# A list scheduler places single instructions of the attention units and weight sums between the feed-forward steps of a fused HGRN2 and bilinear FFN kernel

## The chip, the cores and the metric

The kernel runs on one core of one Trainium2 chip. The metric is the device time of one execution, in microseconds (us). The profile is of one execution on the same kind of core. TensorE is called PE, VectorE DVE, ScalarE ACT, GpSimd POOL and SyncE SP, as the profile does.

## The reference

A gated linear recurrence runs over 4 batches x 8 heads, 768 tokens of 48 channels; its output, 3072 tokens of 384 channels, goes through a bilinear feed-forward block of 1536 inner channels.

```python
f = 1.0 / (1.0 + np.exp(-f_logit))
for t in range(S):
    state = f[:, :, t, :, None] * state + np.einsum('bhd,bhe->bhde', k[:, :, t], v[:, :, t])
    y[:, :, t] = np.einsum('bhd,bhde->bhe', q[:, :, t], state)
x = y.transpose(0, 2, 1, 3).reshape(B * S, H * D)
out = ((x @ w_a) * (x @ w_b)) @ w_out
```

The device computes in float32. The weights arrive as 64-bit numbers and are narrowed on the device.

## The kernel before

**Units.** The recurrence is cut into 16 units: a batch, a half of the tokens (384) and a group of four heads. Two units make a block of 384 tokens x 384 channels, `xT[blk]`, of which there are eight. For a unit, `front` makes the two sigmoids on ACT, an affine step on POOL (line 289), the scans of products of f and of its inverse on DVE (lines 294 and 304), and multiplies q and k by them (306, 307). Then PE and the other engines do `scores` (with a mask on DVE, 357), `turn` (transposes of k, copied out by ACT, 373), `gains` (sums into states by DVE, 405), `within` and `across` (copied out by ACT, 457), and SP's DMAs carry the result into `xT`.

**Feed-forward.** For the first two blocks, `up` makes 12 steps each of 6 matmuls for one 128-wide slice of both inner products, and `product` multiplies the halves. While these run, the 20 pieces of the weights are narrowed (`from_double`). For the other six blocks `up_triples` computes the same by a scheme with 15 products in place of 18 over sums of weights (`combine_w_ba`) and of inputs (`combine_x`): four passes j of 15 products, two matmuls each, into four PSUM banks `ps_f`; ACT copies a bank out (616, 597), or DVE adds it to an earlier copy (619). A bank is used several times in a pass, and its next product waits until the copy or the addition has read it. `down` multiplies two groups of 128 tokens by `w_out` with 7 sub-products in place of 8, over sums of weights (`combine_w_out`: t1 to t4) and of inputs (s1 to s4, by DVE); each sub-product is 6 matmuls, into halves x0, x1, m0, m1 of two banks. There are 12 such calls.

**The order.** All instructions are emitted in one program order by the source, and each engine runs its own in that order; semaphores hold an instruction until what it depends on has finished. The order is written out by hand. `rest` is a list of feed-forward steps; a counter `step` goes up by 1 for an `up` step or a third of a triple pass, and by 0.5 for a sub-product of `down`. A queue of pairs (due step, generator) holds the six parts of each unit's `slot` and the 22 parts of the weight sums; after each step, `beside()` emits the parts that are due, each as a whole. `combine_x` is emitted as a whole in the last `down` ahead of its triples, and `combine_w_out` after the last narrowing.

**The sums of weights.** `combine_w_out` is four DVE additions (674 to 677) into `spare`, where the narrowing kept its bits, and into `w_out`. `combine_w_ba` is six ACT copies (533), eleven DMAs that add on the way (539), issued by POOL, and four DVE additions (547).

Of the kernel before, what the change touches and what calls it, by code (L numbers as in the profile page):

```python
# [19 lines left out]
C = 128  # L20
# [14 lines left out]
def weight_pieces(w_ba, w_out, moe_w_a, moe_w_b, moe_w_out):  # L35

    w_b, w_a = (w_ba[:, i] for i in range(2))
    NKT, NFT, DM = w_ba.shape[2], w_out.shape[1], w_out.shape[2]
    for ft, n in [(0, 1)] + [(ft, 2) for ft in range(1, NFT - 1, 2)] + [(NFT - 1, 1)]:
        for dst, src in ((w_b, moe_w_b), (w_a, moe_w_a)):  # L40
            cols = slice(ft * 128, (ft + n) * 128)
            yield dst[:, :, cols], src.rearrange("(kt p) c -> p kt c", p=128)[:, :, cols], (NKT, n * 128)
    for ft in range(0, NFT, 2):
        rows = moe_w_out[ft * 128:(ft + 2) * 128]
        yield w_out[:, ft:ft + 2], rows.rearrange("(k p) c -> p k c", p=128), (2, DM)
# [84 lines left out]
def by_quotients(ctx, tc, q, k, f_logit, v, moe_w_a, moe_w_b, moe_w_out, out, ident, weights, bad):  # L130
# [89 lines left out]
    todo, raws, going = list(weight_pieces(w_ba, w_out, moe_w_a, moe_w_b, moe_w_out)), [], []  # L220
# [47 lines left out]

    live = {}
# [7 lines left out]
    def front(u):  # L277
# [5 lines left out]
        if u in FIRST:  # L283
            nc.scalar.activation(F, x, AF.Sigmoid)
        nc.scalar.activation(inv, x, AF.Sigmoid, bias=less, scale=-1.0, accum_out=tails[:, u:u + 1])  # L285
        if u not in FIRST:
            nc.scalar.activation(x, x, AF.Sigmoid)

        nc.gpsimd.tensor_scalar(inv, inv, EXP_K, 1.0, ALU.mult, ALU.add)  # L289
        yield  # L290
        none = zero.broadcast_to((128, BLK))
        for n in range(2):
            c = slice(n * BLK, n * BLK + BLK)
            nc.vector.tensor_tensor_scan(F[:, c], F[:, c], none, math.exp(MIDDLE), ALU.mult, ALU.add)
        nc.vector.tensor_tensor(held[:, u], products_of_f[u][:, :, BLK - 1], least, ALU.is_ge)
        yield

        start = sb2.tile([128, 2, NC - 1], FP32, tag="start", name="start")
        nc.vector.reciprocal(start, products_of_f[u].rearrange("p n (c m) -> p n c m", m=C)[:, :, 0:NC - 1, C - 1])
        for n in range(2):  # L300
            for c in range(NC):
                w = slice(n * BLK + c * C, n * BLK + c * C + C)
                first = start[:, n, c - 1:c] if c else math.exp(-MIDDLE)
                nc.vector.tensor_tensor_scan(inv[:, w], inv[:, w], none[:, 0:C], first, ALU.mult, ALU.add)  # L304
        yield
        nc.vector.tensor_tensor(halves(t["q"]), halves(t["q"]), F, ALU.mult)
        nc.vector.tensor_tensor(halves(t["k"]), halves(t["k"]), inv, ALU.mult)
        live[u] = {}
        yield


# [21 lines left out]
    def scores(u, spare=False):  # L333
# [3 lines left out]
        for n, c, o in each():  # L337
            for h in range(2):
                for p in range(2):
# [7 lines left out]
                    )  # L347
        at = sb1.tile([128, 2, BLK], FP32, tag="at", name="at")
# [12 lines left out]
    def turn(u, spare=False):  # L361
# [10 lines left out]
        if not spare:  # L372
            nc.scalar.copy(kT.rearrange("s n c x -> s n (c x)"), ps_x[:, :, 0:BLK])
        live[u]["kT"] = kT
        give_back(ps)

    def gains(u):
# [21 lines left out]
        for j in range(NJ - 1 if last else NJ):  # L399
            c, p = divmod(j, 2)  # L400
            new = ps_x[:, p, 0:2 * NC * D].rearrange("r (n c d) -> r n c d", n=2, c=NC)[:, :, c]
            if before is None:
                nc.vector.tensor_copy(st[:, j], new)
            else:
                nc.vector.tensor_tensor(st[:, j], before, new, ALU.add)
            before = st[:, j]
        before = live[u]["st"][-1]
        if not last:

            for n in range(2):  # L410
                end = products_of_f[u][:, n, BLK - 1:BLK]
                nc.vector.tensor_scalar(before[:, n], before[:, n], end, math.exp(-MIDDLE), ALU.mult, ALU.mult)
# [19 lines left out]
    def across(u):  # L432
# [19 lines left out]
        y = sb1.tile([128, 2 * NC, 2, SUB], FP32, tag="y", name="y")  # L452

        whole = [(0, 0, 0, 128)] if ps[0] is y_banks[0] else [(0, 0, 0, D), (0, R, R, D)]
        for p, e, r, rows in (*whole, (1, R, 0, D), (1, 0, R, D)):
            copy = nc.vector.tensor_copy if u in FIRST and p else nc.scalar.copy
            copy(y[r:r + rows, :, p], ps[p][e:e + rows, 0:BLK].rearrange("r (o m) -> r o m", m=SUB))
        give_back(ps)
        y = y.rearrange("r (n c) p m -> r n (c p m)", n=2)
# [22 lines left out]

    factors = []

    def up(blk, ft):

        x, ps = xT[blk], {}
        for nm, w in (("b", w_b), ("a", w_a)):
            ps[nm] = ps_f[idle.pop(0)]
            for kt in range(NKT):  # L490
                nc.tensor.matmul(  # L491
                    ps[nm][:, 0:BLK],
                    lhsT=w[:, kt, ft * 128:ft * 128 + 128],
                    rhs=x[:, kt],
                    start=kt == 0,
                    stop=kt == NKT - 1,
                )
        factors.append((blk, ft, ps))
# [16 lines left out]
    free = []  # L515

    def combine_w_ba():

# [11 lines left out]
        for to, sign, x in (  # L530
            (s[1], 1, a12), (s[0], 1, a21), (s[3], 1, a22), (s[4], -1, a33), (s[5], -1, a11), (s[2], 1, a12)
        ):
            nc.scalar.activation(to, x, AF.Copy, scale=float(sign))
            yield
        for to, x in (
            (s[1], a22), (s[0], a32), (s[3], a23), (s[4], a31), (s[5], a31), (s[2], a22),
            (s[1], a23), (s[3], a32), (s[4], a21), (s[5], a32), (s[2], a21),
        ):
            nc.gpsimd.dma_start(out=to, in_=x, accum_op=ALU.add)
            yield  # L540
        for to, x, y, op in (
            (a31, a11, a31, ALU.subtract),
            (a31, a31, a33, ALU.add),
            (a22, s[1], a31, ALU.subtract),
            (a22, a22, a13, ALU.add),
        ):
            nc.vector.tensor_tensor(to, x, y, op)
            yield

    def combine_x(blk):  # L550
# [7 lines left out]

        def op(to, x, y, op):
            nc.vector.tensor_tensor(to, x, y, op)  # L560

        op(s[:, 0:2], x[:, 0], b31.unsqueeze(1).broadcast_to((128, 2, HT)), ALU.add)
        op(v1, b21, u5, ALU.subtract)
        op(v6, b31, b21, ALU.subtract)
        op(b11, b11, b12, ALU.subtract)
        op(u1, b11, v6, ALU.add)
        op(r2, b22, b32, ALU.subtract)
        op(v2, b22, v1, ALU.subtract)
        op(v4, b22, b31, ALU.subtract)
        op(t2, b32, b31, ALU.subtract)  # L570
        op(b32, b12, b32, ALU.add)
        op(b21, b21, b22, ALU.subtract)
        nc.scalar.activation(b22, b22, AF.Copy, scale=-1.0)
# [4 lines left out]
        )  # L578

    def up_triples(blk):  # L580
# [3 lines left out]
        def times(ps, name, j, start=False):  # L584
# [9 lines left out]

        def finish(j, c, out, v):
            times(v, "v6", j)
            nc.scalar.copy(out[1, 0], v)
# [3 lines left out]
            nc.vector.tensor_tensor(to.rearrange("p g (k j) t -> p j g k t", k=NI)[:, j], a, b, ALU.mult)  # L601

        for j in range(NJ3):
# [11 lines left out]
            def copy(to, ps):  # L615
                nc.scalar.copy(to, ps)  # L616

            def add(k, i, ps):
                nc.vector.tensor_tensor(out[k, i], ps, out[k, i], ALU.add)  # L619

            times(v, "v1", j, True)
            copy(out[2, 0], v)
            if tail:
                finish(*tail)
            times(u, "u1", j, True)
            copy(out[1, 1], u)
            times(r, "r2", j, True)
            add(1, 1, r)
            times(v, "v2", j)
            copy(out[2, 1], v)  # L630
            times(u, "u2", j)
            copy(first[:, :, 1], u)
            yield
            times(t, "t1", j, True)
            times(v, "v3", j)
            copy(first[:, :, 0], v)
            nc.vector.tensor_tensor(c[:, :, 1:3, 1], c[:, :, 1:3, 1], first, ALU.add)  # L637
            times(u, "u3", j)
            copy(out[0, 1], u)
            times(r, "r3", j, True)  # L640
            add(2, 1, r)
            times(v, "v4", j)
            copy(second[:, :, 1], v)
            yield
            times(u, "u4", j)
            copy(out[0, 0], u)
            add(0, 0, t)
            times(v, "v5", j)
            copy(second[:, :, 0], v)
            nc.vector.tensor_tensor(c[:, :, 0], c[:, :, 0], second, ALU.add)  # L650
            times(u, "u5", j)
            add(2, 0, u)
            times(t, "t2", j)
            add(0, 1, t)
            tail = j, c, out, v
            if j == NJ3 - 1:
                finish(*tail)
            yield

# [672 lines left out]
```

## Time and profile before

| | |
|---|---|
| time, median of three runs | 636.44 us (634.92 to 636.75) |
| the profiled execution: its time, its span | 636.59 us, 634.9 us |
| PE busy in 0 to 80 us | 51.8 us |
| DVE additions 674 to 677 | 1.35, 1.36, 1.36, 1.98 us |
| DVE additions 547 | 4, of 1.22 us |
| DMA additions 539 | 11, 512 KB each, median 10.1 us from issue to landing |
| start of the first `down` sub-product, and of the triples | 147.9 us, 210.8 us |
| last matmul starts, last store is issued | 625.38 us for the last group, 627.97 us |

Span means first to last instruction; some 1.7 us of the execution's time lie outside it. A float32 matmul is recorded as two instructions, so a sub-product of six appears as x12. The rows of a stage table give for each stretch the busy time of each engine; where PE's falls short of the stretch's length, PE was idle. A wait is put down to the instruction that released the one waiting.

### The profile page before, as it was taken

To read this page: it belongs to the slowest core of one execution; us is meant where nothing else is said; L and a number is where in the kernel's file an instruction comes from. 1 tells how busy PE (TensorE), PEld (TensorE's weight loads), DVE (VectorE), ACT (ScalarE), POOL (GpSimd) and SP (SyncE) were. 2 spreads that over 40 slices of the span, in tenths; PEclk is the share of its full clock that TensorE was granted. 3 is DMA by queue.
4 is the path that set the end of the run, shared out by engine and by line. 5 is a ranking of instruction groups with operands and counts; after the bars stand their busy time and mean duration, and the time that the engine had idled before them with its cause. 6 is when DMAs were issued, how large, how long until landed. Compare 5 with 4: busy or idle time off the path is not lost.

```text
span 634.9 us, 13922 instructions
## 1 busy us (share of the span) xinstructions
PE 579.7 (91%) x5778; PEld 512.9 (81%) x5778; DVE 413.6 (65%) x762; ACT 273.6 (43%) x508; POOL 77.0 (12%) x69
## 2 busy tenths in 40 slices
PE   0759899999997999998999999998999999999995
PEld 0626555558997888897999999898999999999995
DVE  6768445487987578757695677847794455745741
ACT  5577499932321445334532255335431245134400
POOL 6244154552000000000000000000000000000000
PEclk9959999999998999999999999999999999999998
DMA  9886775089244403040131404031000100000000
GB/s 215 247 251 174 173 262 185 15 143 189 57 115 90 119 1 95 2 102 18 32 64 40 105 3 94 3 73 46 17 6 33 38 1 20 2 27 1 1 26 30
DMA packets 33337, 49.43 MB, mean 78 GB/s; under 512 B 3952, under 2 KB 25072, under 8 KB 33264
## 3 DMA queue, kind: packets, MB, share of 16 engines
q1 hardware_dynamic: 29984, 42.38, 24.7%
q0 software_dynamic: 2992, 5.77, 5.4%
q8 instruction: 47, 0.77, 0.5%
q10 hardware_dynamic: 288, 0.30, 0.2%
q14 instruction: 26, 0.21, 0.1%
HBM read 33.23 MB, written 4.72 MB: 60 GB/s over the span
## 4 chain that ended last, share of the span: by engine, by line
PE 52%; DVE 11%; ACT 4%; issue 2%; DVEq 0%; ACTq 0%
PE ps_f L586 32%; PE ps_f L697 15%; DVE inv L304 2%; DVE x_sums L560 1%; DVE sums L692 1%; PE ps_x L341 1%; PE ps_y L423 1%; DVE groups L560 1%; PE ps_x L369 1%; DVE sums L637 1%; DVE sums L619 1%; DVE groups L601 1%; ACT inv L285 1%; DVE xT L560 1%; PE ps_y L444 1%
## 5 line engine op out<-in xcount | busy, mean ns | idle before, releaser
L491 PE MATMUL ps_f<-xT,w_ba 128*128 128x384 f32 x288 | 98.4, 502 | 7.8 <-DVE w_ba L66 6.2
L491 PEld LDWEIGHTS ps_f<-xT,w_ba 128*128 128x128 f32 x288 | 55.3, 195 | 47.7 <-DVE w_ba L66 7.3
L616 ACT COPY sums<-ps_f 128x384 f32<-128x384 f32 x108 | 51.8, 480 | 72.0 <-PE ps_f L586 69.0
L616 ACT COPY groups<-ps_f 128x384 f32<-128x384 f32 x108 | 51.7, 479 | 62.8 <-PE ps_f L586 55.1
L586 PE MATMUL ps_f<-xT,w_ba 128*128 128x192 f32 x384 | 78.6, 333 | 0.0
L586 PEld LDWEIGHTS ps_f<-xT,w_ba 128*128 128x128 f32 x384 | 63.4, 190 | 4.8 <-ACT sums L616 2.4
L586 PE MATMUL ps_f<-x_sums,raw 128*128 128x192 f32 x288 | 57.1, 331 | 6.3 <-ACT groups L616 6.2
L586 PE MATMUL ps_f<-groups,w_ba 128*128 128x192 f32 x288 | 55.3, 328 | 4.6 <-DVE sums L619 4.6
L586 PEld LDWEIGHTS ps_f<-x_sums,raw 128*128 128x128 f32 x288 | 46.6, 190 | 9.5 <-ACT groups L616 8.0
L697 PE MATMUL ps_f<-w_out,sums 128*128 128x192 f32 x288 | 53.8, 338 | 0.0
L586 PEld LDWEIGHTS ps_f<-groups,w_ba 128*128 128x128 f32 x288 | 47.8, 190 | 6.4 <-DVE sums L619 6.4
L697 PE MATMUL ps_f<-w_out,groups 128*128 128x192 f32 x288 | 51.1, 327 | 0.6 <-DVE u L692 0.6
L697 PE MATMUL ps_f<-spare,sums 128*128 128x192 f32 x288 | 49.6, 328 | 1.3 <-DVE sums L692 1.2
L289 POOL TENSOR_SCALAR inv<-inv 128x768 f32<-128x768 f32 x14 | 13.7, 975 | 298.3 <-ACT inv L285 298.3
L697 PEld LDWEIGHTS ps_f<-w_out,sums 128*128 128x128 f32 x288 | 48.6, 196 | 0.7
L697 PEld LDWEIGHTS ps_f<-spare,sums 128*128 128x128 f32 x288 | 46.8, 190 | 2.5 <-issue 1.3
L697 PEld LDWEIGHTS ps_f<-w_out,groups 128*128 128x128 f32 x288 | 47.2, 190 | 1.3 <-DVE u L692 1.2
L56 POOL TENSOR_SCALAR sums<-sums 128x768 f32<-128x768 f32 (+1 forms) x20 | 40.9, 2045 | 51.2 <-ACT sums L54 49.4
L619 DVE TENSOR_TENSOR groups<-ps_f,groups 128x384 f32<-128x384 f32 x60 | 32.2, 552 | 17.6 <-ACT groups L616 16.2
L619 DVE TENSOR_TENSOR sums<-ps_f,sums 128x384 f32<-128x384 f32 x60 | 32.1, 551 | 15.1 <-PE ps_f L586 9.9
L586 PE MATMUL ps_f<-x_sums,w_ba 128*128 128x192 f32 x192 | 39.0, 326 | 0.0
L586 PE MATMUL ps_f<-xT,raw 128*128 128x192 f32 x192 | 39.0, 326 | 0.0
(129 smaller groups left out, 869.6 us busy)
## 6 DMA issues: line engine op xcount, KB each, us to landing
raw<-w_ba POOLq DMA_DIRECT2D x11, 512.0 KB, 10.1
q_in<-in_q_dram SPq DMA_DIRECT2D x32, 144.0 KB, 4.2
k_in<-in_k_dram SPq DMA_DIRECT2D x32, 144.0 KB, 3.4
v_in<-in_v_dram SPq DMA_DIRECT2D x16, 288.0 KB, 5.0
raw<-in_moe_w_out_dram SPq DMA_DIRECT2D x6, 768.0 KB, 4.2
out_dram<-o SPq DMA_DIRECT2D x24, 192.0 KB, 1.9
f_in<-in_f_logit_dram SPq DMA_DIRECT2D x28, 144.0 KB, 3.0
xT<-y SPq DMA_DIRECT2D x46, 72.0 KB, 2.2
```

The lines of the kernel that those rows point to most:

```text
L56: nc.gpsimd.tensor_scalar(h, h, HI_MAX, None, ALU.min)
L285: nc.scalar.activation(inv, x, AF.Sigmoid, bias=less, scale=-1.0, accum_out=tails[:, u:u + 1])
L289: nc.gpsimd.tensor_scalar(inv, inv, EXP_K, 1.0, ALU.mult, ALU.add)
L304: nc.vector.tensor_tensor_scan(inv[:, w], inv[:, w], none[:, 0:C], first, ALU.mult, ALU.add)
L341: nc.tensor.matmul(ps[h][SUB * p:SUB * p + SUB, o:o + SUB], lhsT=kf[r, tokens(n, c, p)], rhs=qf[r, tokens(n, c, p)], start=True, stop=True,)
L369: nc.tensor.transpose(ps[n][:, c * C:c * C + C], kf[:, o:o + C], ident)
L491: nc.tensor.matmul(ps[nm][:, 0:BLK], lhsT=w[:, kt, ft * 128:ft * 128 + 128], rhs=x[:, kt], start=kt == 0, stop=kt == NKT - 1,)
L560: nc.vector.tensor_tensor(to, x, y, op)
L586: nc.tensor.matmul(ps[:, g], lhsT=sums_of_w[name][:, g, 128 * j:128 * j + 128], rhs=sums_of_x[blk][name], start=start and g == 0, stop=Tru ...
L616: nc.scalar.copy(to, ps)
L619: nc.vector.tensor_tensor(out[k, i], ps, out[k, i], ALU.add)
L697: nc.tensor.matmul(to, lhsT=x[:, i // 2, i % 2], rhs=w[:, i // 2, i % 2], start=first and i == 0, stop=i == HFT - 1, skip_group_check=True)
```

## The change

The hand-written queue is replaced by a list scheduler in the source. The first 14 up steps and all before them stay. The rest of the feed-forward work becomes a list `main` of single steps (engine, load in ns, due, function): on PE one step is two matmuls of the triples or of a sub-product, or one of an `up`, and `due` names the count of PE steps (beats) by which an ACT or DVE step should be through. Units and sums become five lines of single steps. `fill()` goes through the lines before each step of `main` and emits what fits by a small model of the engines (`now`, `free_at`, a latency of 200 ns), unless `delays` says that a step of `main` on the same engine would then miss its due beat. `emit_until` forces a line up to a mark where `main` needs it.

The order inside a triple pass changes: t1 is copied out early and u4 added to it, and t2 stands ahead of v5. In `down` the sub-products go x0 (a11 b11), m1 (s3 t3), x0 (a12 b21), x1 (s2 t2), m0 (s1 t1), x1 (a22 t4), m0 (s4 b22); before, they went x0, m1, x1, m0, x0, m0 (s4 b22), x1 (a22 t4). The sign of s3 and t3 is turned in both.

The DVE additions of the weights' sums are gone. `combine_w_out` becomes four ACT copies with a sign and five accumulating DMAs; two ACT copies and four accumulating DMAs replace the four DVE additions of `combine_w_ba`. `w_out`'s rows are kept in another order, so that its halves are contiguous.

```diff
@@ weight_pieces
-        yield w_out[:, ft:ft + 2], rows.rearrange("(k p) c -> p k c", p=128), (2, DM)
+        place = w_out.rearrange("p (j k) c -> p k j c", j=apart)
+        to = place[:, ft // apart, ft % apart:ft % apart + 2] if apart > 1 else w_out[:, ft:ft + 2]
+        yield to, rows.rearrange("(k p) c -> p k c", p=128), (2, DM)
@@ sums of weights
+    def add_by_dma(to, x):
+        nc.gpsimd.dma_start(out=to, in_=x, accum_op=ALU.add)
+    def write(to, x, sign):
+        nc.scalar.activation(to, x, AF.Copy, scale=float(sign))
+    def dma_sums(steps, width, issue):
+        for to, x, what in steps:
+            if what in (1, -1):
+                yield ACT, width, 0, write, to, x, what
+            else:
+                yield POOL, issue, 3500 if what == "w" else 0, add_by_dma, to, x
-        nc.vector.tensor_tensor(t1, b12, b11, ALU.subtract)
-        nc.vector.tensor_tensor(t2, b22, t1, ALU.subtract)
-        nc.vector.tensor_tensor(t4, b21, t2, ALU.subtract)
-        nc.vector.tensor_tensor(b12, b12, b22, ALU.subtract)
+        return dma_sums((
+            (t1, b11, -1), (t2, b12, -1), (t1, b12, "w"), (b12, b12, -1), (t2, b11, ""), (b12, b22, ""),
+            (t2, b22, "w"), (t4, t2, -1), (t4, b21, ""),
+        ), 1300, 2500)
-        for to, x, y, op in (
-            (a31, a11, a31, ALU.subtract),
-            (a31, a31, a33, ALU.add),
-            (a22, s[1], a31, ALU.subtract),
-            (a22, a22, a13, ALU.add),
-        ):
+        return dma_sums((
+            (s[1], a12, 1), (s[4], a33, -1), (s[5], a11, -1), (s[1], a22, ""), (s[4], a31, ""), (s[5], a31, ""),
+            (s[3], a22, 1), (s[2], a12, 1), (s[0], a21, 1), (s[1], a23, ""), (s[4], a21, ""), (s[5], a32, ""),
+            (s[3], a23, ""), (s[2], a22, ""), (s[0], a32, ""), (s[3], a32, ""), (s[2], a21, ""),
+        ), 1000, 1300), dma_sums((
+            (a31, a31, -1), (a31, a11, ""), (a31, a33, "w"), (a22, a31, -1), (a22, s[1], ""), (a22, a13, ""),
+        ), 1000, 1300)
@@ up_triples, a pass from t1 on
-            times(t, "t1", j, True)
-            times(v, "v3", j)
...
-            times(u, "u4", j)
-            copy(out[0, 0], u)
-            add(0, 0, t)
-            times(v, "v5", j)
-            copy(second[:, :, 0], v)
...
-            times(t, "t2", j)
-            add(0, 1, t)
+            yield times(t, "t1", j, True)
+            yield copy(6, out[0, 0], t)
+            yield times(v, "v3", j)
...
+            yield times(u, "u4", j)
+            yield add(3, 0, 0, u)
+            yield times(t, "t2", j)
+            yield add(5, 0, 1, t)
+            yield times(v, "v5", j)
+            yield copy(2 if j == NJ3 - 1 else 3, second[:, :, 0], v)
@@ down
+        yield from times(x0, a11, b11, True)
+        yield on(ACT, 330, 4, begin)
+        s1, s2 = block(), block()
+        yield add(10, s1, a21, a22)
+        yield add(7, s2, s1, a11, ALU.subtract)
+        yield from times(m1, s3, t3, True)
+        yield on(ACT, 330, 7, second)
+        yield from times(x0, a12, b21)
+        yield on(ACT, 330, 7, third)
+        s4 = block()
+        yield add(10, s4, a12, s2, ALU.subtract)
+        yield from times(x1, s2, t2)
+        yield on(DVE, 270, 4, sum_u2)
+        yield on(DVE, 270, 0, sum_u3)
+        yield from times(m0, s1, t1)
+        yield on(DVE, 270, 4, last_of, 1, 1, m0)
+        yield from times(x1, a22, t4, True)
+        yield on(DVE, 270, 8, last_of, 1, 0, x1)
+        yield on(SP, 0, 0, store, 1)
+        yield from times(m0, s4, b22)
+        yield on(DVE, 270, 4, last_of, 0, 1, m0)
+        yield on(SP, 0, 0, store, 0)
@@ the scheduler
+        def delays(engine, start, load):
+            with_it, without = start + load, free_at[engine]
...
+            for ready, cost, due in later:
+                if ready >= with_it:
+                    return False
+                with_it, without = (max(x, ready) + cost for x in (with_it, without))
+                if with_it + LATENCY > max(starts.get(due, 1 << 30), without + LATENCY):
+                    return True
+            return False
+        def fill():
+            more = True
+            while more:
+                more = False
+                for line in lines:
+                    start = earliest(line)
...
+                    if engine == PE:
+                        fits = start <= now
+                    else:
+                        start = max(start, free_at[engine])
+                        fits = start <= now + BEAT and not delays(engine, start, load)
+                    if fits:
+                        emit(line, start)
...
+        for done, (engine, load, due, do, *args) in enumerate(main):
+            if done in beside:
+                emit_until(*marks[beside[done]])
+                if beside[done] == ("x", 2):
+                    emit_until(*marks["ba"])
+            fill()
...
+            do(*args)
```

`begin`, `second` and `third` are the ACT copies u2 from x0, c21 from m1 and c11 from x0. In the changed kernel, ACT's sign copies stand at line 602, the accumulating DMAs at 599, the matmuls of the triples at 687 and of the down products at 780, and the copies `begin`, `second` and `third` at 797, 804 and 807.

## The prediction

> **What bounds the kernel now.** I read the page's busy shares and slices first, then busy time by stage, then what TensorE waited for, then VectorE's and GpSimd's work around the step from the first phase to the second. Page and stage table (columns: PE, PEld, DVE, ACT, POOL busy us with counts, granted clock, DMA share, GB/s):
>
> ```profile
> PE 579.7 (91%) x5778; PEld 512.9 (81%) x5778; DVE 413.6 (65%) x762; ACT 273.6 (43%) x508; POOL 77.0 (12%) x69
> 127.00:147.50 20.50, 20.50 (x92) 12.01 (x94) 15.17 (x22) 7.96 (x14) 11.54 (x10) 1.00 0.91 154
> 147.50:167.50 20.00, 19.72 (x279) 18.74 (x272) 18.51 (x36) 3.63 (x7) 3.08 (x3) 1.00 0.77 142
> 167.50:211.00 43.50, 39.74 (x624) 37.46 (x623) 33.90 (x75) 12.59 (x25) 1.67 (x2) 0.92 0.34 85
> 211.00:320.00 109.00, 101.92 (x1105) 96.32 (x1104) 76.55 (x144) 48.07 (x100) 2.50 (x3) 1.00 0.23 56
> 320.00:500.00 180.00, 173.30 (x1870) 165.24 (x1868) 126.04 (x236) 64.46 (x136) 3.53 (x4) 1.00 0.16 41
> 500.00:627.50 127.50, 125.75 (x842) 121.83 (x842) 66.88 (x107) 42.85 (x94) 0.00 (x0) 1.00 0.04 14
> ```
>
> TensorE sets the time: full from 127 to 147.5, and never under 91% later. All that better order can win is its idle time: 109 - 101.9 + 180 - 173.3 + 127.5 - 125.8 = 15.5 us after 211, where the triples begin, and 0.3 + 3.8 us before. What it waited for from 211 to 628 (us, times, longest), and the one long wait earlier, from the timeline:
>
> ```profile
> PE ps_f L586 <- ACT groups L616: 6.2, 5, 1.2
> PE ps_f L586 <- DVE sums L619: 4.6, 6, 0.9
> PE ps_f L697 <- ACT o L732: 3.3, 5, 0.7
> PE ps_f L697 <- DVE sums L692: 1.2, 4, 0.7
> ```
>
> ```profile
> 200.36 1.65 PE L341 MATMUL ps_x<-q_in,k_in 48*64 48x64 f32 x48 [3.24 <-DVE k_in L307]
> ```
>
> These are matmuls whose PSUM bank or sum is late because a sigmoid or a scan of a unit stood ahead on ACT or DVE: what a list scheduler can remove. After the 3.24 us the clock falls to half (0.51 from 200 to 205, 0.81 to 210), which costs (0.49 + 0.19) x 5 = 3.4 us.
>
> The third thing is the accumulating DMAs of line 539, from GpSimd's timeline and the DMA view of 136 to 160:
>
> ```profile
> 123.86 2.64 POOL L539 DMA_DIRECT2D raw<-w_ba  x2 [1.87 <-ACT raw L533]
> 133.23 7.36 POOL L539 DMA_DIRECT2D raw<-w_ba  x6
> 146.07 3.69 POOL L539 DMA_DIRECT2D raw<-w_ba  x3
> q0 software_dynamic: 2306, 4.45, 110.5%
> ```
>
> They issue quickly but move slowly: in those 24 us the 16 DMA engines are full (110.5%). Of 2306 packets 135 are small; 2171 / 24 = 90 packets a us, and one addition has 256, so each takes **2.83 us** of all engines. The eleven ran from about 125.8 to 161. Nobody waited, since the triples need them only at 211.
>
> **What the Trainium skill says.** "DMA: Bandwidth & Descriptors", section "SWDGE vs HWDGE vs iDMA": accumulation in a DMA goes through GpSimd's software queue alone, of which one is allocated; the trace agrees, all eleven are in q0. Same page, "Issuing engines are not separate DMA queues": all queues end on the same 16 engines; the full engines above agree, so further additions line up. Same page, "Anatomy of one DMA — SWDGE (gpsimd) path": about 2.0 us + bytes / 436e3, which is 3.2 us for 512 KB. The trace disagrees: 5.4 us from issue to landing at best, median 10.1; I use the trace. "TensorE: Matmul & The Clock Gate", "What's actually happening": about 3.4 us idle halves the clock; the drop after 3.24 us agrees.
>
> **The change part by part.** Matmul counts are equal (144 up, 720 triple, 504 down, 1568 of the units), so TensorE's work stays. The conversions and first 14 up steps are as before; their hand-over at about 126 is common.
>
> *w_out's combinations.* Removed: four DVE additions (3 x 1.36 + 1.98 = 6.0 us, lines 674 to 677). No gain: they ran at 128 to 134 while TensorE was full. Added: four sign copies on ACT (1152 columns, about 1.17 us from 1.05 for 1024) and five accumulating DMAs of 576 KB in 768-byte runs, a form not in the trace. Bounds: by bytes 2.83 x 576/512 = 3.2 us; at a full packet's price per run (768 against 256) 8.5 us. Plain packets of 1024, 2048 and 3072 bytes took medians of 53, 84 and 121 ns in the DMA records, so 768 would be near half of 2048: 3 x 0.49 x 2.83 = 4.1. I take 3.75, between.
>
> *w_ba's combinations.* Four DVE additions (4.9 us, line 547) become two ACT copies and four DMAs of 2.83 us. Twenty additions now stand on one queue instead of eleven. The order of the changed kernel shows who waits: on ACT the copy a22 = -a31 waits for the 18th addition (a31 += a33), which is issued only when the 17th has landed; and **behind that copy on ACT stands the copy u2 of the second down product**, without which TensorE cannot go to its third sub-product.
>
> *When the 18th lands.* First copy t1: ACT is free of x_sums at 126.3, +1.17 = 127.5. Issue to first packet, as before, 125.8 - 123.9 = 1.9: 129.4. Then 13 x 2.83 + 5 x 3.75 = 55.6; the second addition's copies aren't ready until 1 us after the first is through; 17th to 18th exposes 0.4 landing + 1.9 issue: 188.3. A unit's loads now fall into it (q, k, f twice 144 KB, v 288 KB, 1.18 MB; q1 moved 42.38 MB in 24.7% of 634.9 us of all engines, so 3.7 us a MB, 4.4 us): I take 3.5, as a part will fall into gaps. Landed 192. Copy 1.1, u2 0.4: TensorE resumes at **T = 193.6**. Without waits it would have been there at 147.5 + 2.5 (the first unit's scores, turn, gains) + 13.7 (7 sub-products) + 4 (units between) + 3.9 (two more) + 0.9 = 172. On the way it already waits some 2 us (u2 behind t4 = -t2 on ACT) and 4 us (t4 itself); these only eat into the same 20 us.
>
> *From T to the triples:* 12 sub-products of 6 matmuls x 1.95 (623.43 to 625.38 in the timeline) = 23.4, two units' matmuls and one `within` about 6.7: 30.1. The long idle halves the clock again, 3.4. In the new order x1 = s2*t2 follows x0 += a12*b21 in the same bank, and the listed wait on ACT stands before it, for the copy `third`. In the last down product before, such a copy began 0.2 us after the matmuls had issued, 0.32 long: about 0.55 us a time (bound 0 if it waits for something earlier), twice here. Triples begin at 193.6 + 30.1 + 3.4 + 1.1 = 228.2 against 211.0: **17.2 us lost**. GpSimd too is held (the inv affine of a unit stands behind these issues), but TensorE's next scores come 16 us after T, when that is past.
>
> *After 211.* Single unit instructions between steps with due steps, and u4/t2/v5/u5 reordered so that each bank has three steps or more to its reuse, should clear most of the 6.2 + 4.6. Left: 9 x 0.55 = 5 of the new down order and some 3 elsewhere, 8 of 15.5: **7.5 gained** (bounds 3.5 and 12.5). The tail is as before: last sum, last store.
>
> Sum: +17.2 - 7.5 = +9.7 on the profiled 636.6 (span 634.9 + 1.7 around it, which stays; the median shown is 636.4): **646**.
>
> **Rivals.**
> - *Chain just covered:* additions by bytes, no loads in the way: T = 193.6 - 2.8 - 3.5 = 187.3, 10.9 lost, 10.5 to 12.5 gained: 635 to 637. For it: the byte-like plain packets. Against: 1.18 MB does have to load for the next unit.
> - *Short runs dear:* 8.5 us each, T + 24: 670. For it: accumulating packets are dearer than plain ones; against: nothing shows a fixed part that large.
> - *Faster:* GpSimd's additions land before the down products ask for them, so that ACT's copy never holds u2. Then the 3.24 + 3.4 us at 200 go too, and 7.5 us or more later: 622. For it: SBUF additions could overlap more than seen, and before nobody waited for them. Against: it needs 18 additions in about 42 us, 2.3 each, where full engines gave 2.83. It decides at T near 184 (9.7 less): beyond, slower.
> - *Scheduler doesn't do what it says:* its table books 1.3 us of GpSimd and 3.5 us to landing for an addition and no DMA engine time, so its order around the copies is that of a shorter chain; this is inside my first case.
>
> **How the numbers follow.** Forecast case 0.74 (own range 638 to 660: T from 187 with 3.2 us a run to 201 with 5 us, twice the clock loss and 4.5 us gained), just covered 0.08, dear runs 0.06, faster 0.12. About 0.3%, 2 us, is what can be told from no change. Faster 0.12 + 0.02, same 0.04 + 0.01, slower the rest, 0.81. Range 636 to 659.
>
> **What would show it.** Right: TensorE idle more than 12 us between 175 and 195, released by ACT's u2 copy (line 797) whose ACT waited for a DMA into w_ba; DMA engines full from 129 to about 190; half clock after; triples (line 687) from about 228; line 780 waiting on ACT `o` about 0.5 us a time; under 10 us of other TensorE idle after it. Wrong: triples begin before 212, or the additions through by 180, or more than 15 us idle later on.

## The result

Four executions of the changed kernel had a median of 647.32 us (646.62 to 648.38), beside 636.56 us (634.92 to 636.75) for four of the kernel before: a ratio of 1.0176, 95% interval 1.0154 to 1.0198. The change makes the kernel 1.8% slower. The forecast was 646.

The page of the changed kernel and its stage table (the columns are those of the table before):

```profile
PE 579.9 (90%) x5778; PEld 514.2 (80%) x5778; DVE 401.2 (62%) x754; ACT 275.9 (43%) x514; POOL 87.3 (14%) x78
127.00:147.50 20.50, 20.50 (x159) 12.39 (x157) 9.55 (x18) 15.16 (x21) 9.06 (x7) 1.00 0.94 139
147.50:167.50 20.00, 15.27 (x176) 12.68 (x166) 15.84 (x32) 5.20 (x9) 11.04 (x9) 1.00 1.15 168
167.50:190.00 22.50, 12.93 (x190) 11.97 (x190) 10.26 (x24) 2.22 (x4) 5.53 (x5) 0.85 1.04 195
190.00:211.00 21.00, 13.23 (x185) 12.32 (x186) 6.38 (x13) 5.79 (x11) 3.28 (x4) 0.76 0.59 109
230.00:320.00 90.00, 87.49 (x1142) 82.08 (x1141) 70.21 (x142) 40.87 (x86) 3.79 (x4) 1.00 0.30 76
320.00:500.00 180.00, 176.41 (x1813) 169.82 (x1812) 124.84 (x232) 68.28 (x148) 2.50 (x3) 1.00 0.14 36
```

TensorE's work is the same (579.9 us for 579.7). But between 147.5 and 211 it is idle for 4.7 + 9.6 + 7.8 = 22.1 us, where before it was idle for 0.3 + 3.8. In the same stretch the DMA share is above 1 until 190 (before it was 0.77, then 0.34): the 16 DMA engines have no room left. From 230 on the idle time is small.

What TensorE waited for, over the whole run (us in total, times, longest), and then the places in its timeline (start, length, instruction, and in brackets the idle time ahead of it and who ended it):

```profile
PE ps_f L780 <- ACT u L797: 17.4, 2, 15.3
PE ps_f L780 <- ACT o L807: 7.7, 12, 1.1
PE ps_f L780 <- DMA spare<-w_out: 3.9, 1, 3.9
```

```profile
157.43 2.22 PE L780 MATMUL ps_f<-w_out,groups 128*128 128x192 f32 x12 [2.10 <-ACT u L797]
169.13 1.24 PE L780 MATMUL ps_f<-spare,groups 128*128 128x192 f32 x4 [3.86 <-DMA spare<-w_out]
...
197.36 3.62 PE L780 MATMUL ps_f<-w_out,groups 128*128 128x192 f32 x12 [15.30 <-ACT u L797]
...
231.86 0.81 PE L687 MATMUL ps_f<-x_sums,raw 128*128 128x192 f32 x4
...
636.57 2.11 PE L780 MATMUL ps_f<-w_out,sums 128*128 128x192 f32 x12
```

Three stalls of 2.1, 3.9 and 15.3 us, all in the first two down products, and the triples begin at 231.86 in place of 210.84: 21.0 us late. The last group of matmuls starts at 636.57 in place of 625.38, 11.2 us late. So 9.8 us were won after the triples' start: 404.7 us from it to the last group, for 414.5 before.

Why the copy of line 797 was late is on ACT's timeline, and why that was late on GpSimd's:

```profile
196.05 1.06 ACT L602 ACTIVATE w_ba<-w_ba 128x1024 f32<-128x1024 f32 x1 [19.51 <-DMA w_ba<-w_ba]
197.01 0.30 ACT L797 COPY u<-ps_f 128x192 f32<-128x192 f32 x1
```

```profile
176.91 1.21 POOL L599 DMA_DIRECT2D w_ba<-w_ba  x1
188.89 1.19 POOL L599 DMA_DIRECT2D w_ba<-w_ba  x1 [10.77 <-DMA w_ba<-w_ba]
197.40 1.19 POOL L599 DMA_DIRECT2D w_ba<-raw  x1 [7.33 <-ACT u L797]
202.69 1.19 POOL L599 DMA_DIRECT2D w_ba<-w_ba  x1 [4.09 <-DMA w_ba<-raw]
```

The sign copy a22 = -a31 stood on ACT for 19.5 us. It waited for the addition issued at 188.89, and that one had waited on GpSimd for the landing of the one before it, issued at 176.91. Directly behind the sign copy, at 197.01, comes the small copy that TensorE needs.

### The profile page after: what moved, and what is told of

It is laid out like the page before. It is cut to its first block, busy times and chain, and to the rows that moved or that the text cites. A ratio compares the mean times of both kernels' runs of the same rounds, so it can differ in the third digit from the quotient of the medians.

```text
span 645.1 us, 13880 instructions
## 1 busy us (share of the span) xinstructions
PE 579.9 (90%) x5778; PEld 514.2 (80%) x5778; DVE 401.2 (62%) x754; ACT 275.9 (43%) x514; POOL 87.3 (14%) x78
## 3 DMA queue, kind: packets, MB, share of 16 engines
q0 software_dynamic: 8000, 10.81, 10.8%
## 4 chain that ended last, share of the span: by engine, by line
PE 72%; DMA 11%; DVE 7%; issue 4%; ACT 3%; SPq 1%; POOL 1%; ACTq 0%; DVEq 0%; POOLq 0%
PE ps_f L687 35%; PE ps_f L780 19%; PE ps_f L567 11%; DMA spare<-w_out 5%; DMA xT<-y 2%; DVE sums L679 2%; DVE groups L679 2%; PE ps_x L423 1%; PE ps_y L466 1%; PE ps_y L487 1%; PE ps_x L364 1%; PE ps_x L399 1%; DMA w_ba<-w_ba 1%; DMA raw<-in_moe_w_a_dram 1%; DVE x_sums L671 1%
## 5 line engine op out<-in xcount | busy, mean ns | idle before, releaser
L1166 ACT COPY sums<-ps_f 128x384 f32<-128x384 f32 x120 | 57.5, 479 | 70.5 <-PE ps_f L687 65.7
L1166 ACT COPY groups<-ps_f 128x384 f32<-128x384 f32 x120 | 57.6, 480 | 67.7 <-PE ps_f L687 45.8
L780 PE MATMUL ps_f<-w_out,groups 128*128 128x192 f32 x288 | 53.4, 335 | 17.4 <-ACT u L797 17.4
L780 PEld LDWEIGHTS ps_f<-w_out,groups 128*128 128x128 f32 x288 | 48.5, 195 | 18.8 <-ACT u L797 18.0
L780 PE MATMUL ps_f<-spare,sums 128*128 128x192 f32 x288 | 51.1, 332 | 7.7 <-ACT o L807 7.7
L780 PEld LDWEIGHTS ps_f<-spare,sums 128*128 128x128 f32 x288 | 46.3, 190 | 11.4 <-ACT o L807 11.2
L687 PE MATMUL ps_f<-x_sums,raw 128*128 128x192 f32 x288 | 53.8, 331 | 0.8 <-DVE sums L679 0.4
L780 PEld LDWEIGHTS ps_f<-w_out,sums 128*128 128x128 f32 x288 | 47.1, 190 | 0.5
L679 DVE TENSOR_TENSOR sums<-sums,groups 128x768 f32<-128x768 f32 x36 | 34.4, 954 | 21.0 <-ACT groups L1166 20.4
```

The source lines that it names most:

```text
L687: nc.tensor.matmul(ps[:, g], lhsT=sums_of_w[name][:, g, 128 * j:128 * j + 128], rhs=sums_of_x[blk][name], start=start and g == 0, stop=Tru ...
L780: nc.tensor.matmul(to, lhsT=x[:, i // 2, i % 2], rhs=w[:, NI * (i % 2) + i // 2], start=start and i == 0, stop=i == HFT - 1, skip_group_ch ...
L1166: do(*args)
```

## The experiments

They ran on three chips, on each beside the kernel before, which took a median of 635.4 to 637.1 us there. What is compared is each one's ratio to it. Differences in us below are a difference of ratios times 636.

Three theories. **A**: the loss is the wait of one copy, placed ahead of a down product's copy on ACT; elsewhere the chain of additions would be hidden. **B**: twenty additions fill the 16 DMA engines for some 60 us, and so slow other transfers too; wherever the copy stands, something else waits. **C**: VectorE had to be freed for the scheduler to place the units, so additions put back on it would cost time.

### The sign copy later

```diff
+                behind["latest", blk] = len(main)
...
-        marks["ba"] = for_ba.extend(w_over, past=behind[1])
+        w_over = list(w_over)
+        for_ba.extend(w_over[0:3], past=behind[1])
+        marks["ba"] = for_ba.extend(w_over[3:], past=behind["latest", 1] - 16)
```

> Only the place of one ACT copy and of the two additions after it changes: a22 = -a31 is emitted late in the third down product instead of ahead of the second one's copy u2. Theory A (the copy waits in ACT's queue for the 18th addition and so holds u2 and TensorE): TensorE's wait on u2 falls from 17.4 to about 2 us, the half clock after it goes too (3.4 us), 647.3 - 15.3 - 3.4 = 628 to 630 us; the DMA engines stay full until about 196 us. Theory B (the full DMA engines themselves hold up the stage, through loads and sums that are late for everyone): the stall moves to t1 in the first triples, 642 us or more.

Measured: 638.05 us, ratio 1.004 (1.002 to 1.006). That is 8.6 us better than the changed kernel; A's forecast was missed by 8 to 10 us. The wait on the copy of line 797 is down to 2.1 us. ACT's timeline shows what came in its place:

```profile
183.32 0.32 ACT L804 COPY o<-ps_f 128x192 f32<-128x192 f32 x1 [5.50 <-DMA out_dram<-o]
...
189.05 0.93 ACT L294 ACTIVATE inv<-f_in,less 128x768 f32<-128x768 f32 x1 [5.19 <-DMA f_in<-in_f_logit_dram]
```

ACT now stands 5.5 us for a store that has not yet left its buffer and 5.2 us for a unit's load. Both are ordinary transfers in the queue of SP. The store is the clearer sign of B: with all sums on VectorE (a run below) ACT waits 1.5 us for a store in this part of the kernel, but 11.2 us, in three times, for loads.

TensorE itself now has short waits in place of the long one. The clock fell after each of the four longest, of 2.1 to 2.7 us. The stage table of this run:

```profile
190.00:211.00 21.00, 18.90 (x251) 17.87 (x252) 16.48 (x38) 5.83 (x13) 2.18 (x2) 0.84 0.55 130
211.00:235.00 24.00, 21.35 (x368) 19.53 (x367) 13.12 (x31) 8.89 (x17) 3.24 (x3) 0.87 0.57 124
```

From 147.5 on the granted clock of the four stretches is 0.91, 0.93, 0.84 and 0.87; with all sums on VectorE it is 1.00, 0.92, 1.00 and 1.00. The missing shares times the lengths are at most 9.9 us for 1.8 (an estimate, as TensorE wasn't busy all the time). A's forecast had the half clock go together with the long wait. So A explains a part of the loss. The next runs are about the rest.

### The sums back on VectorE: of w_ba, of w_out, of both

The four DVE additions of before, as single steps of the same scheduler:

```diff
-        dma_sums(((a31, a31, -1), (a31, a11, ""), (a31, a33, "w"), (a22, a31, -1), ...), 1000, 1300)
+        ((DVE, 1220, 0, nc.vector.tensor_tensor, to, x, y, op) for to, x, y, op in (
+            (a31, a11, a31, ALU.subtract), (a31, a31, a33, ALU.add),
+            (a22, s[1], a31, ALU.subtract), (a22, a22, a13, ALU.add)))
```
```diff
-        return dma_sums(((t1, b11, -1), (t2, b12, -1), (t1, b12, "w"), ...), 1300, 2500)
+        return ((DVE, 1360, 0, nc.vector.tensor_tensor, to, x, y, ALU.subtract) for to, x, y in (
+            (t1, b12, b11), (b12, b22, b12), (t2, b22, t1), (t4, b21, t2)))
```

Of w_ba alone (16 additions by DMA are left):

> The last four sums of w_ba go back to four DVE additions; 16 accumulating DMAs are left. Theory A: the same 15.3 + 3.4 us go as in the first run, 628 to 630 us, though fewer bytes move. Theory B: clearly better than the first run, as 4 x 2.83 us of DMA time go. Theory C (DVE's lost time matters): 4.9 us of DVE work comes back and costs 2 us or more against the first run.

Measured: 630.74 us, 0.9937 (0.9917 to 0.9957). That is A's number or nearly so, but also B's "clearly better than the first run", by 6.6 us. C is out: with more work on VectorE the kernel is faster. TensorE still waits 2.2 and 3.8 us in the first down product for w_out's sums.

Of both (11 are left, as before):

> All sums that DVE had before are back on DVE; 11 accumulating DMAs are left, as in the kernel before. Theory A: the waits on t4 = -t2 (2.1 us) and t4 (3.9 us) in the first down product go as well, and with them the last half clock there: 621 to 624 us, which is what the scheduler and the two orders are worth alone, 12 to 15 us under the kernel before. Theory C (the additions had to leave DVE for the scheduler to fit the units): no better than the second run.

Measured: 622.32 us, 0.9799 (0.9763 to 0.9835). This is as A forecast (621 to 624), though one fall of the clock stays (0.92 from 167.5 to 190, after a wait of 3.0 us), and C is out again. Where the triples and the last group begin:

```profile
211.53 0.81 PE L691 MATMUL ps_f<-x_sums,raw 128*128 128x192 f32 x4
...
613.03 2.11 PE L784 MATMUL ps_f<-w_out,sums 128*128 128x192 f32 x12
```

Against the changed kernel that is 20.3 us at the triples' start and 3.2 us after it: **the nine additions by DMA, with the six sign copies on ACT that belong to them, cost 24 us** (1.0176 - 0.9799), and without them the rest of the change makes the kernel faster by 2%.

Of w_out alone (15 are left):

> The counterpart of the second run: w_out's sums on DVE, w_ba's last four by accumulating DMAs as changed, 15 in all. The same ACT copy a22 = -a31 still stands ahead of the second u2, but waits for the 13th addition, 5 x 4.1 us less in the queue: it lands at about 176 us in place of 196, so the wait on u2 is 3 to 6 us in place of 15.3: 626 to 630 us. Theory A's simple form (the copy's place costs 15 us whatever stands before it in the DMA queue): 638 us or more.

Measured: 635.91 us, 1.0016 (1.0001 to 1.0031): 6 us off the forecast. TensorE's waits there:

```profile
PE ps_y L466 <- ACT y L512: 7.0, 1, 7.0
PE ps_f L781 <- ACT o L808: 6.5, 11, 0.9
PE ps_x L423 <- ACT kT L409: 5.0, 2, 4.8
```

The sign copy got its data at about 171.7, but here it held up ACT's copies of a unit's output (line 512). SP sends that output on, and behind it, in SP's order, come the next unit's loads and a store; then a unit's kT stood on ACT behind a down product's copy that waited 4.7 us for this store. I had reckoned only with the one copy behind the sign copy, not with what stands behind it in other queues.

Each half of the sums costs on its own: w_out's five additions 8.8 us (0.9937 - 0.9799), w_ba's four 13.8 us (1.0016 - 0.9799); together 22.6, against 24.0 for both at once.

How much of that is slower transfers? The DMA view of 150 to 197, for transfers that nobody changed (how many, KB each, median us from issue to landing; q0 is the additions' queue with packets, MB and share of the 16 engines). The changed kernel:

```profile
q0 software_dynamic: 4445, 6.53, 87.6%
out_dram<-o SPq DMA_DIRECT2D x2, 192.0 KB, 6.4
xT<-y SPq DMA_DIRECT2D x3, 72.0 KB, 7.7
```

With all additions of the change back on VectorE:

```profile
q0 software_dynamic: 1340, 2.57, 32.2%
out_dram<-o SPq DMA_DIRECT2D x4, 192.0 KB, 4.0
xT<-y SPq DMA_DIRECT2D x6, 72.0 KB, 2.2
```

With w_out's alone on VectorE:

```profile
q0 software_dynamic: 2304, 4.42, 56.8%
xT<-y SPq DMA_DIRECT2D x6, 72.0 KB, 2.1
```

With twenty additions they took 87.6% of all 16 engines in these 47 us, and a transfer of 72 KB of a unit's result needed 7.7 us in place of 2.2. B's slowing is real there. But with 15 additions such a transfer took 2.1 us, and with 16 (w_ba's alone on VectorE) 2.2, and those kernels still lose 13.8 and 8.8 us. Slowed transfers can explain little of these two losses. What the traces show is in-order queues in which something stands for an addition: with 15 the sign copy on ACT, with 16 the copy t4 = -t2 on ACT and the sum t4 itself.

The runs give one way to split the 24 us: 8.6 go when the sign copy is moved, 6.6 more when w_ba's additions are on VectorE altogether (1.004 - 0.9937), and the last 8.8 are w_out's. Only the middle part is left for B, and it also holds the falls of the clock that follow the short waits; how much of it is slowed transfers is not shown.

### The scheduler told the true price

```diff
-        ), 1300, 2500)
+        ), 1300, 4100)
...
-        ), 1000, 1300), dma_sums((
+        ), 1000, 3000), dma_sums((
...
-        ), 1000, 1300)
+        ), 1000, 3000)
```

The additions of w_out had been booked at 2.5 us, those of w_ba at 1.3; the 3.5 us to landing stay as they were.

> The changed kernel with only the scheduler's table altered: an accumulating DMA is booked with about the time that it takes (3.0 us for 512 KB, 4.1 us for 576 KB in short runs) in place of 1.3 us. It then puts the copies a31 = -a31 and a22 = -a31 into the third down product, behind several more of ACT's copies; the copies t4 = -t2 and the additions are the same. Theory A, the stall came from a wrong price in the planner: the 15 us wait of the second down product's copy goes, and the time is 634 to 640, as when the copy was moved by hand (638.1), since the DMA engines stay full and hold loads and stores. Rival: with true prices for all steps the units' loads and products are placed well too, and nearly the whole 25 us that the additions by DMA cost comes back, 622 to 630. Second rival: forced steps ahead of the triples now wait for the chain's end in one piece, 643 or more.

Measured: 649.56 us, 1.0213 (1.0183 to 1.0243). The second rival came in: no better than the changed kernel. TensorE's waits from 120 to 236, and the places on GpSimd's timeline behind them:

```profile
PE ps_f L687 <- DMA w_ba<-w_ba: 8.6, 1, 8.6
PE ps_f L687 <- DVE x_sums L671: 6.8, 1, 6.8
```

```profile
183.85 1.19 POOL L599 DMA_DIRECT2D raw<-w_ba  x1 [3.63 <-DMA raw<-w_ba]
197.75 0.82 POOL L297 TENSOR_SCALAR inv<-inv 128x768 f32<-128x768 f32 x1 [12.71 <-ACT inv L294]
198.63 1.22 POOL L599 DMA_DIRECT2D raw<-w_ba  x1
...
222.25 1.20 POOL L599 DMA_DIRECT2D w_ba<-w_ba  x1 [4.10 <-DMA w_ba<-raw]
```

The stall in the second down product is gone, as A would have it, and the triples' first matmul runs at 210.94. But it had waited 6.8 us for a sum of inputs (VectorE had stood for the transfer xT<-y), and soon after it the triples stand 8.6 us until the last addition lands at 227.3. The chain had been held up on GpSimd itself: a unit's affine step (line 297) stood between two additions and waited 12.7 us for its sigmoid on ACT, which waited for its load. That load was issued late: five transfers ahead of it in SP's queue took 7.8 us to issue (3.1 us in the changed kernel at 209, when its additions are through). So the additions delay SP's transfers, a load behind these delays the affine, and the affine delays the additions.

The affine step before that one waited still longer, with no transfer to blame:

```profile
174.44 0.82 POOL L297 TENSOR_SCALAR inv<-inv 128x768 f32<-128x768 f32 x1 [14.35 <-ACT inv L294]
```

Its sigmoid waited for VectorE, and VectorE waited for no transfer. Ten of the 20 additions stood behind this step, and from 170 to 176 the DMA engines were all but empty (share 0.01). So the higher price has a cost of its own: the table books an addition as work of GpSimd, which spaces the additions out and lets affine steps in between, and its model has no DMA engines that loads and stores share. That a dearer booking on GpSimd doesn't help is shown; what a model with DMA engines would win was not tried.

### The order of the down products

The rest of `down` after `second`, in the order of before; all else as in the changed kernel, and once more with all sums on VectorE:

```diff
-        yield from times(x0, a12, b21)
-        yield on(ACT, 330, 7, third)
...
         yield from times(x1, s2, t2)
...
         yield from times(m0, s1, t1)
         yield on(DVE, 270, 4, last_of, 1, 1, m0)
-        yield from times(x1, a22, t4, True)
-        yield on(DVE, 270, 8, last_of, 1, 0, x1)
-        yield on(SP, 0, 0, store, 1)
+        yield from times(x0, a12, b21)
+        yield on(ACT, 330, 4, third)
         yield from times(m0, s4, b22)
...
+        yield from times(x1, a22, t4, True)
+        yield on(DVE, 270, 4, last_of, 1, 0, x1)
+        yield on(SP, 0, 0, store, 1)
```

> The changed kernel with the sub-products of a down product in the order of the kernel before (x0, m1, x1, m0, x0, m0, x1); all else, the sums by DMA too, as changed. If the wait of x1 = s2 t2 on the copy of x0 in the same bank is the cause of TensorE's 7.7 us on ACT o (12 times about 0.64), it falls below 2 us and the time by some 5.5 us, the share of it that lies outside the stalled stage: 641 to 642 us. Rival (the other order loses as much on DVE sums, as the kernel before lost 3.3 + 1.2 us there): 645 to 648 us.

Measured: 640.58 us, 1.0092 (1.0058 to 1.0125), 5.3 us better than the changed kernel. TensorE's longest waits:

```profile
PE ps_f L780 <- ACT o L804: 11.9, 3, 11.1
PE ps_f L780 <- DVE sums L679: 5.5, 6, 3.3
PE ps_f L780 <- ACT u L797: 2.1, 1, 2.1
```

The waits on line 807 are gone, as forecast, and the time is near the forecast. But in the profiles the triples begin 4.3 us earlier (227.61 for 231.86), so more of the gain lies in the stalled stage than after it, where I had put it. The long stall is now on the copy of line 804, 11.1 us, behind the same sign copy on ACT: the order of the products only chooses which copy stands there.

> All sums on DVE as in the third run, and the sub-products of a down product in the order of the kernel before. In the third run TensorE waited 9.3 us on the copy of x0 (ACT o), 3.0 of them once behind a copy of kT. If both parts add, these fall below 2 us: 615 to 617 us, 19 us under the kernel before. Rival: the adjacent s2 and m0 then wait for DVE instead, as DVE has the sums again: 620 us or more.

Measured: 618.68 us, 0.9753 (0.9699 to 0.9806), 2.9 us better than with the new order, though the two intervals overlap; the forecast was 615 to 617. The waits of the down products' matmuls are 5.5 us (3.3 on ACT's copies, 2.2 on VectorE's sums) in place of 9.3 us on ACT's copies. This is the fastest of all: 2.5% below the kernel before, with the scheduler, the new triples, and no new addition by DMA.

### The order of the triples, and the scheduler alone

Both with all sums on VectorE; in a pass, t1, u4, v5, u5 and t2 are emitted in the order of before:

```diff
             yield times(t, "t1", j, True)
-            yield copy(6, out[0, 0], t)
...
             yield times(u, "u4", j)
-            yield add(3, 0, 0, u)
-            yield times(t, "t2", j)
-            yield add(5, 0, 1, t)
+            yield copy(2, out[0, 0], u)
+            yield add(3, 0, 0, t)
             yield times(v, "v5", j)
...
             yield times(u, "u5", j)
+            yield add(4, 2, 0, u)
+            yield times(t, "t2", j)
+            yield add(4, 0, 1, t)
```

> All sums on DVE as in the third run, and a triple pass in the order of the kernel before (u4 copied, t added to it, v5, u5, then t2): two steps from u4 to u5 where the new order has three. If the spacing of the bank reuses is part of what the change gains after 211 us, TensorE's waits in the triples rise from under 1 to 3 us or more: 624 to 627 us. If the list scheduler's due steps alone do it: 622 us as the third run.

Measured: 627.8 us, 0.9895 (0.9851 to 0.9938), 6.1 us slower than with the new triples. The time is as forecast or a little above, but TensorE's own waits on the triples' copies did not grow: they show 0.2 us. What grew are its waits on the down products' copy of line 811, from 5.5 to 7.5 us after 211, and a unit's transposes wait 1.4 us for a mask; the two profiled executions differ by 2.7 us only (625.93 and 623.22). The weight loads, which run ahead of the matmuls, show some of it. First all sums on VectorE with the new triples, then with the old, from 211 to 630:

```profile
PEld ps_f L784 <- ACT o L811: 8.2, 9, 1.2
PEld ps_f L691 <- ACT sums L1170: 1.7, 6, 0.5
```

```profile
PEld ps_f L784 <- ACT o L811: 10.1, 9, 2.2
PEld ps_f L691 <- ACT groups L1170: 2.9, 12, 0.5
PEld ps_f L691 <- ACT sums L1170: 2.6, 12, 0.2
```

The load's waits on the triples' copies rise from 1.7 us (6 times) to 5.5 us (24 times), each half a us at most. Those on line 811 rise by 1.9. How much of a load's wait becomes time of the matmul behind it, the records don't say; that the 6.1 us are these waits is likely, not shown.

With the old down order as well, the scheduler is left, and with it the new order of w_out's rows:

> The changed kernel with all sums of weights back on DVE and with both orders, of the down products and of the triples, as they were before: of the change the list scheduler alone is left. If the parts simply add, from the runs so far (all additions on DVE 622.3, with the old down order 618.7, with the old triple order 627.8): 622.3 - 3.6 + 5.5 = 624, so that the scheduler alone wins some 12 us and the two orders nearly cancel. Rival: the scheduler and the new triple order need each other (its due beats are drawn up for banks that have three steps to their reuse), so the old triples cost more than 5.5 us here, 628 or more. A second rival: the old down order makes the old triples cheap, 620 or less.

Measured: 624.84 us, 0.981 (0.9779 to 0.9842). The parts add as in the first forecast (624): the list scheduler alone wins 1.9%, 12 us. The new triples give about 0.6% more (0.9753 against 0.981, with the old down order; the intervals just overlap), and the new down order takes back 0.5 to 0.9%.

## Why the prediction was right

The direction, the place and the size came out; the runs support the mechanism but widen it.

- *When TensorE resumes:* T = 193.6 was forecast, 197.36 measured. The addition that ACT waited for landed at 196.0, not 192, within 7% of the chain's 63 us. One part is the last link: 188.89 to 196.0 is 7.1 us from issue to landing, where the next addition, issued at 197.40 to idle engines, took 5.0. A unit's loads were in its way: from 188 to 197 SP's queue took 56.7% of the 16 engines' time and the addition 31.9%. My 3.5 us were for loads alone: from 150 to 197 SP's transfers took 16.7% of all engines, 7.8 us, with stores and units' results that I had left out. The term of 3.75 us for runs of 768 bytes was somewhat low too: the median accumulating packet (one record of a DMA engine) of 768 bytes took 93 ns. Packets of 2048 bytes show 191 ns where 2.83 us an addition allow 177, a factor of 1.08; so 768 x 93 / 16 engines / 1.08 = 4.1 us, an estimate, and 1.8 us more for five.
- *The earlier stalls:* 2 and 4 us forecast, 2.1 and 3.86 measured, at the two places named.
- *From T to the triples:* 34.6 us forecast with the clock's share and the waits on `third`, 34.5 measured (231.86 - 197.36). That it fits so well is in part luck. The clock cost less than my 3.4 us: the first group of twelve took 3.62 us for 2.11, 1.5 us, and after 200 the clock was 0.98. The waits on `third` were 0.41 and 1.12. So the units' matmuls took 34.5 - 23.4 - 1.5 - 1.5 = 8.1 us, where I had 6.7. The clock also fell once before, to 0.50 from 170 to 172, after the 3.86 us.
- *Triples' start:* 17.2 us lost by forecast, 21.0 measured, nearly all of the difference from T.
- *After 211:* 7.5 us gained by forecast, 9.8 measured. Idle time was 15.5 us; now it is 404 - 396.3 = 7.7 between 228 and 632, so 7.8 is the part that was forecast. The other 2 us are no gain: as much of TensorE's work moved ahead of the triples' start (after it TensorE is busy for 399.1 us, before 401.1). The waits on `third` are 5.7 us in nine times (forecast 5 in nine); elsewhere about 2 us are left and not 3.
- *The sum:* +9.7 forecast; the profiled matmuls end 11.2 later, the medians differ by 10.8. Two errors, +3.8 and -2.3, partly cancelled.
- *The rivals:* "faster" needed T near 184, 13 us earlier than it came. Its price was good, though: 622 if no addition held up TensorE, and with the sums on VectorE 622.3 was measured. Runs of 768 bytes at 8.5 us are excluded by the packets. That the scheduler's table is wrong was part of my forecast case; it is wrong, but the run with the higher price shows that booking more time on GpSimd doesn't help.
- *What the prediction didn't say:* it made nearly the whole loss a matter of one chain and one copy behind it; the two earlier stalls, it said, "only eat into the same 20 us". But moving that copy won back 8.6 us of 24, and w_out's additions, which make the earlier stalls, cost 8.8 us by themselves. It also left out the other direction of what the Trainium skill states in "DMA: Bandwidth & Descriptors", "Issuing engines are not separate DMA queues", that all queues interleave on the same 16 engines: I counted how the units' loads slow the additions, not how the additions slow SP's transfers. The trace agrees with the page, 7.7 us for 2.2 on 72 KB, where all twenty additions are by DMA. And it took about 3.4 us of idle time for a fall of the clock; waits of 2.1 to 2.7 us were enough when the copy had been moved.

## What to carry to other kernels

An engine with idle time is not the only cost of moving work off a busy one: eight VectorE additions that nobody waited for (10.9 us) became nine DMAs more on a queue of eleven, which then took 88% of all DMA engines for 47 us and delayed other transfers. When a chain of such transfers is long, ask for each in-order queue what stands behind the instruction that waits for it, and then what the shared engines delay in other queues. The shared engines need not be full for a loss: with 15 additions a unit's result moved as fast as with none of the new ones, and 13.8 us were still lost. Test the parts of a rewrite one by one: here a scheduler worth 2% lay under a change that cost 4%.

## What the runs showed of the hardware

- The median packet of 2048 bytes took 191 ns where it accumulated from SBUF to SBUF, and 84 ns in plain loads of the weights from HBM. No plain SBUF-to-SBUF transfer with packets of that size ran, so how much of the difference is the accumulation is not shown.
- Shorter runs cost an accumulating DMA little extra: 768 bytes took 93 ns, which is 0.121 ns a byte for 0.093 at 2048 bytes.
- How long the half clock lasts was not in proportion to the idle time: after 15.3 us idle TensorE worked at half clock for about 2.8 us more (0.50 to 200, 0.98 to 205), after 3.24 us in the kernel before for some 6.8 us (0.51 and 0.81 in the two stretches of 5 us from 200).
- The clock fell to half after gaps of 2.12, 2.46, 2.54 and 2.65 us in the run with the sign copy later (0.50 in 158 to 160, 167.5 to 170.5, 191.5 to 198 and 229 to 235), and not after 2.10 us in the changed kernel (1.00 from 157 to 160) or 2.15 us in the run with w_ba's sums alone on VectorE (1.00 from 157 to 161).
- SP takes longer to issue while the DMA engines are full: five transfers xT<-y took it 7.3 us from 178.07 in the changed kernel (DMA share 1.04 from 167.5 to 190), and 3.1 us from 209.04 (share 0.17 from 207 to 212.2).
